# Attention scores from one product of 64 partitions per head, in two banks, in place of one product of two heads against keys in a block with zeros

## The chip, the cores and the metric

The kernel runs on one core of a Trainium2 chip. The metric is device time in microseconds (us) of one execution, and the figure of a kernel is the median of several runs. A second, profiled execution gives the trace: one record for each instruction of TensorE (PE for the products, PEld for its weight loads), VectorE (DVE), ScalarE (ACT), GpSimd (POOL) and for each transfer.

## The reference

Three stages follow each other: attention over keys and values that are averaged in groups of 8, a gated feed-forward block (moe) with a norm, and a second feed-forward block (moe2). Only the first is touched by the change.

```python
batch, n_heads, seq, head_dim = (4, 8, 576, 64)          # q, k, v
def _attn_ref(q, k, v):
    pool = 8; Sp = S // pool                              # 72 pooled positions
    scale = 1.0 / np.sqrt(D)
    k_p = k.reshape(B, H, Sp, pool, D).mean(axis=3)
    v_p = v.reshape(B, H, Sp, pool, D).mean(axis=3)
    scores = scale * np.matmul(q, k_p.transpose(0, 1, 3, 2))
    scores = scores - np.max(scores, axis=-1, keepdims=True)
    attn = np.exp(scores)
    attn = attn / (np.sum(attn, axis=-1, keepdims=True) + 1e-09)
    return np.matmul(attn, v_p)
# then moe on 2304 tokens x 512 (hidden 1536), then moe2 of the same sizes
```

## The kernel before

The 2304 tokens are cut into 18 sub-tiles of 128 tokens for the attention (`sub_steps(s)`). One batch has 576 tokens, so sub-tiles 4 and 13 hold the end of one batch in their first 64 rows and the beginning of the next in the other 64. The feed-forward block works on token tiles of 512, 256, 768 and 768, and its many products of 128 x 128 weights fill TensorE from about 36 us to the end. The attention of the later sub-tiles is strewn between them.

Pooled keys. For each batch `k_pool(p)` (L320) sums the keys of head pair p in groups of 8 into `kp` (DVE, 128 partitions: two heads of 64 dimensions each). `k_blocks(hh)` (L331) then copies the rows of one head of every pair, times 1/8, into `KB`, a tile of 128 x 4 x 144: rows 0 to 63 hold the first head of each pair in columns 0 to 71, rows 64 to 127 the second in columns 72 to 143, and the rest are zeros that GpSimd writes once at the start (L226). Two such tiles take turns over the batches.

Scores. `scores` (L407) makes one product for each head pair: the stationary operand is the queries of the pair (128 partitions x 128 tokens), the moving one the 144 columns of `KB`. So 4 products fill a sub-tile's 576 scores, pairs 0 and 1 in one PSUM bank, pairs 2 and 3 in the next. A straddling sub-tile makes 4 products for its first 64 tokens and 4 for the others. Each product in f32 shows in the trace as two instructions of weight load and product, so an ordinary sub-tile has 8 of each. Behind the scores DVE takes the maximum of each head (`top`, L434) and, from sub-tile 4 on, subtracts it (L436). In sub-tiles 0 to 3 TensorE subtracts it instead (`less`, L440). ACT takes the exponent (L452), and TensorE transposes the result (`turn`, L459).

Order. The order on the compute engines is written out by hand: `FIRST` and `SECOND` are lists of tokens, and each token issues one step. `S5.0` is the scores of sub-tile 5, `S5.1` the maximum, `S5.2` the exponent, `k0` to `k3` are `k_pool` of batch 0, `b0` and `b1` its `k_blocks`; `p`, `r` and `u` are the same steps of batches 1 to 3 (0 to 3 `k_pool`, 4 to 6 the values, 7 and 8 `k_blocks`, 9 the values' blocks). A `!` moves a step to another engine. Within one engine the instructions run in this order, whatever is ready. `laid_out` arranges the inputs on the host: it decides which two heads form a pair.

Of the kernel before, what the change touches and what calls it, by code (L numbers as in the profile page):

```python
# [45 lines left out]
Y10l! W11c M1.ca Fb00l W11l! S11.10 V11b O10a H11 M1.la! S11.11 S11.12 Y11c Y11l O10b Fd0 M0.la!
M0.e1! S12.2 S13.0 Ft1c M0.e2! O11a T1 S13.1 T0 Fd2 O11b T2 S13.2 M0.e3 T3 || S13.3 M0.1 M0.cs Ft1l
M1.1 M0.ls! M0.e4 M0.2 M1.e1 u9 S13.4 S12.3 M0.cr Fd1 Ft3c M0.p5 S12.4 M1.e2 M0.3 M0.lr! M1.3 M0.p1
Ft2c Fd3 Ft2l S13.5 M1.cs M0.cb M1.ls! M0.4 M1.2 Fb11c M1.p1 Ft3l Fb11l M2.ca M0.u2 M1.e4! M1.e3!
M2.la S13.6 M1.cr Ft4c M0.7 M0.d3 M0.d1 M1.4 M0.lb M1.lr! Ft4l M1.d1 S12.5 M2.e1! M1.u2 M0.5 M0.z1  # L50
M1.p5 S12.6 M2.3 M1.7 M2.e2! M1.6 M0.d2 M0.d5 M1.5 M2.cs M2.1 M2.e3 M1.cb M0.z2 M3.ca S14.0 M2.e4!
M2.ls! M0.d4 M3.e1! M1.lb! M2.2 M2.cr M1.z1 M1.d3 M2.p1 M2.6 M2.p5 M3.la! M3.e2! M3.cs M3.3 M2.4
M4.ca M1.d2 M1.d5 M2.d1 M2.lr M2.cb M3.1 M2.5 M2.u2 M2.lb M3.ls! M2.7 M3.e3 S14.1 M3.e4 M2.z1
M4.e1! M1.z2 M3.2 M4.e2! M4.la M2.d2 M3.cr M3.p1 M2.d3 M2.z2 M3.6 M3.d1 M3.z1 M1.d4 M4.cs S15.0
M2.d5 M4.3 M3.4 M3.lr! M4.1 M3.p5 M4.e4 M3.cb S15.1 M4.e3! S14.2 M4.cr M5.ca M3.u2 M4.ls! M3.lb
M2.d4 M5.e1 M4.lr! S14.3 M5.e2 M3.5 M4.2 M5.e3! S15.2 M4.p1 M3.d2 M3.7 M5.cs M3.d3 M4.d1 M5.e4
M4.p5 M3.z2 M5.ls M4.4 M6.ca M4.6 M5.la! M4.5 M3.d5 M5.3 M5.cr M6.la M5.2 M6.e1 M4.u2 S12.7 M6.e2!
# [96 lines left out]
def attention_moe_moe2(  # L154
# [1509 lines left out]
```

## Time and profile before

| | us |
|---|---|
| runs | 957.96, 960.32, 960.05 |
| median | 960.05 |
| the profiled execution | 960.59 |
| its span, first to last instruction | 958.9 |
| PE busy in the span | 933.3 |
| DVE busy | 631.6 |
| ACT busy | 485.6 |
| granted TensorE clock, mean | 0.994 of full |

The profiled execution took 960.59 us, of which 958.9 are the span and 1.7 lie around it. Engines overlap, so busy times don't add up to the span. A product's record reaches from its start to the modelled end of its way through the array; the next one may start long before that. The distance between two starts is therefore the better measure of what one product takes.

### The profile page before, as it was taken

To read this page: it belongs to the slowest core of one execution; us is meant where nothing else is said; L and a number is where in the kernel's file an instruction comes from. 1 tells how busy PE (TensorE), PEld (TensorE's weight loads), DVE (VectorE), ACT (ScalarE), POOL (GpSimd) and SP (SyncE) were. 2 spreads that over 40 slices of the span, in tenths; PEclk is the share of its full clock that TensorE was granted. 3 is DMA by queue.
4 is the path that set the end of the run, shared out by engine and by line. 5 is a ranking of instruction groups with operands and counts; after the bars stand their busy time and mean duration, and the time that the engine had idled before them with its cause. 6 is when DMAs were issued, how large, how long until landed. Compare 5 with 4: busy or idle time off the path is not lost. (4 is left out here: it accounts for less than half of the span.)

```text
span 958.9 us, 14761 instructions
## 1 busy us (share of the span) xinstructions
PE 933.3 (97%) x5242; PEld 854.0 (89%) x5242; DVE 631.6 (66%) x1119; ACT 485.6 (51%) x941; POOL 310.9 (32%) x291
## 2 busy tenths in 40 slices
PE   7899999999999999999989999999999999999998
PEld 6786676999999998999978899999999998888886
DVE  5889664778877867767856798766666675232221
ACT  3776643867675644666645565444434444322211
POOL 3312412653555322254322205443333433400000
PEclk9999999999999999999999999999999999999999
DMA  8577623543011163521474434344444336553431
GB/s 296 204 212 247 213 94 110 165 127 102 29 50 50 53 184 116 168 97 58 134 240 146 133 107 154 128 135 135 135 154 140 127 116 230 179 165 99 159 105 66
DMA packets 67945, 133.35 MB, mean 139 GB/s; under 512 B 7456, under 2 KB 31264, under 8 KB 67872
## 3 DMA queue, kind: packets, MB, share of 16 engines
q1 hardware_dynamic: 67728, 132.28, 42.4%
q8 instruction: 41, 0.67, 0.3%
q14 instruction: 32, 0.26, 0.1%
q10 hardware_dynamic: 144, 0.13, 0.0%
HBM read 93.06 MB, written 39.32 MB: 138 GB/s over the span
## 5 line engine op out<-in xcount | busy, mean ns | idle before, releaser
L1188 DVE TENSOR_TENSOR hl<-hf,hh 128x768 fp32r<-128x768 f32 x36 | 35.0, 976 | 91.7 <-ACT hh L1187 91.7
L1210 PE MATMUL o<-woh,hh 128*128 128x512 f32 x216 | 84.0, 389 | 0.0
L1210 PE MATMUL o<-wol,hh 128*128 128x512 f32 x216 | 84.0, 389 | 0.0
L1210 PE MATMUL o<-woh,hl 128*128 128x512 f32 x216 | 84.0, 389 | 0.0
L1187 ACT CAST hh<-hf 128x768 fp32r<-128x768 f32 x36 | 30.0, 839 | 85.3 <-PE o L1210 76.8
L1543 PE MATMUL o<-hh,wol 128*128 128x256 f32 (+1 forms) x192 | 66.0, 344 | 3.2 <-ACT hh L1527 1.9
L1543 PE MATMUL o<-hl,woh 128*128 128x256 f32 (+1 forms) x192 | 65.4, 340 | 1.1 <-DVE hl L1530 1.1
L1543 PE MATMUL o<-hh,woh 128*128 128x256 f32 (+1 forms) x192 | 65.4, 341 | 0.0
L647 POOL TENSOR_TENSOR w<-w,st 128x512 int32<-128x512 int32 x20 | 26.2, 1312 | 114.9 <-DVE w L640 68.7
L1115 ACT COPY p<-X 128x384 f32<-128x384 f32 x36 | 17.3, 481 | 88.1 <-PE X L1107 88.1
L679 POOL TENSOR_TENSOR wl<-wf,wh 128x512 fp32r<-128x512 f32 x26 | 34.7, 1340 | 56.6 <-ACT wh L675 55.5
L1210 PEld LDWEIGHTS o<-woh,hl 128*128 128x128 f32 x216 | 40.5, 188 | 8.5
L1210 PEld LDWEIGHTS o<-wol,hh 128*128 128x128 f32 x216 | 40.5, 188 | 8.4
L617 ACT ACTIVATE st<-st 128x512 int32<-128x512 uint32 x72 | 48.0, 667 | 0.0
L1210 PEld LDWEIGHTS o<-woh,hh 128*128 128x128 f32 x216 | 40.5, 188 | 8.3
L1543 PEld LDWEIGHTS o<-hh,wol 128*128 128x128 f32 x192 | 36.8, 192 | 8.0 <-ACT hh L1527 2.4
L697 PE MATMUL acc<-ht,wo 128*128 128x512 f32 (+1 forms) x112 | 43.5, 531 | 0.0
L647 POOL TENSOR_TENSOR wo<-wo,st 128x512 int32<-128x512 int32 x16 | 21.8, 1362 | 64.7 <-ACT p L1115 24.9
L1107 PE MATMUL X<-xh_t,rl 128*128 128x384 f32 x120 | 40.6, 338 | 1.6 <-ACT u L1115 1.6
L1543 PEld LDWEIGHTS o<-hl,woh 128*128 128x128 f32 x192 | 36.7, 191 | 5.8 <-DVE hl L1530 1.6
L1107 PE MATMUL X<-xh_t,sl 128*128 128x384 f32 x120 | 40.8, 340 | 0.5 <-ACT p L1115 0.5
L1143 DVE TENSOR_TENSOR u<-u,Y 128x384 f32<-128x384 f32 x36 | 19.8, 550 | 32.4 <-ACT u L1115 15.3
(255 smaller groups left out, 3160.8 us busy)
## 6 DMA issues: line engine op xcount, KB each, us to landing
hf<-h SPq DMA_DIRECT2D x36, 384.0 KB, 3.1
st<-in_moe_w_out_dram SPq DMA_DIRECT2D x24, 512.0 KB, 3.9
h<-p SPq DMA_DIRECT2D x60, 192.0 KB, 1.9
h<-u SPq DMA_DIRECT2D x60, 192.0 KB, 1.9
wo_again<-wd SPq DMA_DIRECT2D x36, 256.0 KB, 2.8
st<-in_moe_w_gate_dram SPq DMA_DIRECT2D x12, 512.0 KB, 4.0
st<-in_moe_w_val_dram SPq DMA_DIRECT2D x12, 512.0 KB, 4.3
wd<-wo SPq DMA_DIRECT2D x24, 256.0 KB, 2.1
```

The lines of the kernel that those rows point to most:

```text
L617: nc.scalar.activation(out=low, in_=low.bitcast(U32), func=AF.Copy, scale=2.0 ** -29)
L647: (nc.vector if boot["alt"] else nc.gpsimd).tensor_tensor(out=bits, in0=bits, in1=low, op=ALU.add)
L679: (nc.vector if boot["alt"] else nc.gpsimd).tensor_sub(wl, wf[ph, f, i], wh.bitcast(F32))
L697: nc.tensor.matmul(accs[c][:, cols], w[:, c, :], ht[:, :cols.stop - cols.start], start=(f == 0 and cols.start == 0), stop=(f == NF - 1),)
L1107: nc.tensor.matmul(dst[:, :HALF], w[:, c0 + c, :], x[:, c, :], start=(start and i == 0), stop=(stop and i == 5), skip_group_check=True,)
L1115: nc.scalar.copy(t, src[:, :HALF])
L1143: nc.vector.tensor_add(u2, u2, Y[:, :HALF])
L1187: nc.scalar.copy(hh, hf)
L1188: nc.vector.tensor_sub(hl, hf, hh.bitcast(F32))
L1210: nc.tensor.matmul(accs[i], x[:, sub], y, start=(f == 0 and j == 0), stop=(f == NF - 1 and j == 2),)
L1543: nc.tensor.matmul(dst, w[:, c, :], x, start=(f == 0 and j == 0 and at == 0), stop=(f == NF - 1 and j == 2), skip_group_check=True,)
```

## The change

Queries and pooled keys of one pair stay in one tile of 128 partitions, the first head of the pair in rows 0 to 63, the second in rows 64 to 127. For each pair and each of the two heads there is now a product of its own with 64 partitions: 128 tokens of stationary queries, 72 moving columns. The first head's scores go to bank 0, the second's to bank 1. A pair is now made of heads p and p + 4, not 2p and 2p + 1, which `laid_out` arranges, so that heads 0 to 3 are bank 0 as before. `KB` has no zeros any more and is half as large; `k_pool` writes it directly. `kp`, `k_blocks` (8 steps over the four batches) and the two clears on GpSimd are gone. The factor 1/8 moves into the scale of the exponent. A number that pads a pool of on-chip memory changes from 120 to 88 words.

```diff
-q0 K K K K K w0! k0 k1 k2 W q1 K k3 K q2 b1 b0 G S0.0@att S0.1 S1.0@acc0 S1.1 S0.8 l S1.8
+q0 K K K K K w0! k0 k1 k2 W q1 K k3 K q2 G S0.0@att S0.1 S1.0@acc0 S1.1 S0.8 l S1.8 S0.2a w1 t0!
...
-    QK_SCALE = 1.0 / float(D) ** 0.5
+    QK_SCALE = 1.0 / (POOL * float(D) ** 0.5)
...
     for i in range(2):
-        t = const.tile([P, NP, 2 * SP], F32, tag=f"KB{i}", name=f"KB{i}")
-        nc.gpsimd.memset(t, 0.0)
-        KB.append(t)
+        KB.append(const.tile([P, NP, SP], F32, tag=f"KB{i}", name=f"KB{i}"))
...
         def k_pool(p):
-            if p == 0:
-                box["kp"] = sm_p.tile([P, NP, SP], F32, tag="kp", name=f"kp_{b}")
             t, _ = queue.pop(p)
             v3 = t.rearrange("p (s r) -> p s r", r=POOL)
-            nc.vector.reduce_sum(out=box["kp"][:, p, :], in_=v3, axis=AX.X)
+            nc.vector.reduce_sum(out=KB[b % 2][:, p, :], in_=v3, axis=AX.X)
             load()
...
-        def k_blocks(hh):
-            rows = slice(hh * D, (hh + 1) * D)
-            dst = KB[b % 2][rows, :, hh * SP:(hh + 1) * SP]
-            if hh == 0 or b > 0:
-                nc.scalar.mul(dst, box["kp"][rows], 1.0 / POOL)
-            else:
-                nc.vector.tensor_scalar_mul(dst, box["kp"][rows], 1.0 / POOL)
...
                 for p in range(2 * b0, 2 * b1):
-                    c0 = (p % 2) * 2 * SP
-                    nc.tensor.matmul(
-                        box["sc"][off:off + cnt, p // 2, c0:c0 + 2 * SP],
-                        q_t[s][:, p, off:off + cnt], KB[b % 2][:, p, :],
-                        start=(s >= BOOT or p % 2 == 0), stop=(s >= BOOT),
-                        skip_group_check=True,
-                    )
+                    for i in range(2):
+                        rows = slice(i * D, (i + 1) * D)
+                        nc.tensor.matmul(
+                            box["sc"][off:off + cnt, i, p * SP:(p + 1) * SP],
+                            q_t[s][rows, p, off:off + cnt], KB[b % 2][rows, p, :],
+                            start=(s >= BOOT or p == 0), stop=(s >= BOOT),
+                            skip_group_check=True,
+                        )
...
-        shift(x_p, 120)
+        shift(x_p, 88)
```

From `FIRST` and `SECOND` only the tokens of `k_blocks` are taken out (`b0 b1`, `p7 p8`, `r7 r8`, `u7 u8`; what was 9 is now 7). No other token moves.

At the start, DVE before: the four sums of batch 0 (L329), one of the two block copies (L341; the other stands on ACT), then the negative identity and the first maximum.

```order
L329 TENSOR_REDUCE kp_140<-kv_6_127 128x72 [waits DMAHW1_49]
L329 TENSOR_REDUCE kp_140<-kv_5_129 128x72 [waits DMAHW2_49]
L329 TENSOR_REDUCE kp_140<-kv_xl 128x72 [waits DMAHW3_49]
L329 TENSOR_REDUCE kp_140<-kv_xl 128x72 [waits DMAHW4_49]
L341 TENSOR_SCALAR KB_105<-kp_140 64x4x72 [waits DVE_49,Pool_49]
L212 TENSOR_SCALAR nident<-ident 128x128 [waits Pool_49]
L434 TENSOR_REDUCE m_182<-sc_175 128x8 [waits PE_49]
```

And DVE after:

```order
L324 TENSOR_REDUCE KB_105<-kv_6_125 128x72 [waits DMAHW1_49]
L324 TENSOR_REDUCE KB_105<-kv_5_127 128x72 [waits DMAHW2_49]
L324 TENSOR_REDUCE KB_105<-kv_xl 128x72 [waits DMAHW3_49]
L324 TENSOR_REDUCE KB_105<-kv_xl 128x72 [waits DMAHW4_49]
L211 TENSOR_SCALAR nident<-ident 128x128 [waits Pool_49]
L421 TENSOR_REDUCE m_181<-sc_170 128x8 [waits PE_49]
```

The sums now write the keys' tile themselves, and the copy between is gone; what follows is the same.

TensorE at sub-tile 13, which straddles two batches, before: the end of one output product of the feed-forward block, the scores (64 tokens against the keys of one batch, 64 against the other's), and the next output product.

```order
L1361 MATMUL acc_1650<-hl_2434,woh_10_2398 128x256
L412 MATMUL sc_2495<-KB_105,q_1972 64x144 [waits DMAHW6_49,PE_49,Activation_49]
L412 MATMUL sc_2495<-KB_105,q_1972 64x144 x3
L412 MATMUL sc_2495<-KB_107,q_1972 64x144 x4
L1361 MATMUL acc_1560<-hh_2480,wol_11_2452 128x256 [waits Activation_49]
L1361 MATMUL acc_1560<-hh_2480,woh_11_2451 128x256
```

And TensorE after, at the same place:

```order
L1347 MATMUL acc_1675<-hl_2476,woh_10_2441 128x256
L399 MATMUL sc_2537<-KB_105,q_2008 64x72 [waits DMAHW6_49,PE_49,Activation_49]
L399 MATMUL sc_2537<-KB_105,q_2008 64x72 x7
L399 MATMUL sc_2537<-KB_106,q_2008 64x72 x8
L1347 MATMUL acc_1587<-hh_2522,wol_11_2494 128x256 [waits Activation_49]
L1347 MATMUL acc_1587<-hh_2522,woh_11_2493 128x256
```

Each product of 144 columns has become two of 72; its neighbours and its waits are the same. An ordinary sub-tile differs in the same way (4 rows of 128x144 become 8 of 128x72).

## Rows read from the trace of the kernel before

**Rows 1.** Page, parts 1 and 2: PE busy us, share, count; tenths in 40 slices.

```profile
PE 933.3 (97%) x5242; PEld 854.0 (89%) x5242; DVE 631.6 (66%) x1119; ACT 485.6 (51%) x941; POOL 310.9 (32%) x291
...
PE   7899999999999999999989999999999999999998
```

**Rows 2.** Stretches: length, busy us (count) by engine, granted clock, DMA share, GB/s.

```profile
12.00:36.00 24.00, 20.24 (x111) 17.42 (x112) 17.69 (x40) 15.39 (x36) 7.34 (x7) 0.86 0.66 234
36.00:100.00 64.00, 60.53 (x308) 47.65 (x307) 57.45 (x103) 46.02 (x79) 16.37 (x13) 1.00 0.74 236
...
170.00:250.00 80.00, 78.62 (x638) 77.38 (x638) 65.95 (x130) 59.51 (x118) 43.23 (x44) 1.00 0.38 114
250.00:350.00 100.00, 99.42 (x609) 98.28 (x608) 77.17 (x158) 62.67 (x129) 43.22 (x46) 1.00 0.20 66
```

**Rows 3.** Instructions of tile sc: count, ns min/median/max, first and last start, forms.

```profile
L412 PE MATMUL sc<-KB,q x160: 283/286/448, 8.8 to 323.7; 128*128 128x144 f32 x128, 128*64 128x144 f32 x32
```

**Rows 4.** PE timeline at sub-tile 12: start us, us, instruction, count.

```profile
225.89 0.28 PE L689 MATMUL v<-xl,wh 128*128 128x256 f32 x1
226.01 1.15 PE L412 MATMUL sc<-KB,q 128*128 128x144 f32 x8
226.90 0.38 PE L689 MATMUL g<-xh,wl 128*128 128x256 f32 x1
227.11 0.28 PE L689 MATMUL g<-xh,wh 128*128 128x256 f32 x1
```

**Rows 5.** PEld timeline, two weight loads of 128 columns before products of 65.

```profile
34.07 0.30 PEld L482 LDWEIGHTS av<-VB,eT 128*128 128x128 f32 x2 [0.59 <-ACT eT L464]
```

**Rows 6.** PE timeline at sub-tile 13, which straddles two batches.

```profile
233.31 0.28 PE L1361 MATMUL acc<-hh,woh 128*128 128x256 f32 x1
233.43 0.28 PE L1361 MATMUL acc<-hl,woh 128*128 128x256 f32 x1
233.63 1.74 PE L412 MATMUL sc<-KB,q 128*64 128x144 f32 x16
235.30 0.38 PE L1361 MATMUL acc<-hh,wol 128*128 128x256 f32 x1
235.53 0.28 PE L1361 MATMUL acc<-hh,woh 128*128 128x256 f32 x1
```

**Rows 7.** PEld timeline, sub-tile 4: the weight loads in flight at 41.67 to 41.70.

```profile
41.65 0.14 PEld L412 LDWEIGHTS sc<-KB,q 128*64 128x64 f32 x2
```

**Rows 8.** PE timeline, scores of sub-tiles 0 to 2 [idle before <- releaser].

```profile
8.79 1.25 PE L412 MATMUL sc<-KB,q 128*128 128x144 f32 x8 [0.32 <-ACT KB L339]
12.03 1.79 PE L412 MATMUL sc<-KB,q 128*128 128x144 f32 x8 [1.99 <-DMA q<-in_q_dram]
...
18.01 1.25 PE L412 MATMUL sc<-KB,q 128*128 128x144 f32 x8
```

**Rows 9.** PE timeline, places where PE waits behind scores.

```profile
43.72 0.52 PE L518 MATMUL xP<-ident,x 128*128 128x128 f32 x3 [0.87 <-DVE x L511]
...
74.29 0.50 PE L689 MATMUL g<-xh,wl 128*128 128x512 f32 x1 [1.31 <-ACT ht L788]
...
164.84 0.36 PE L689 MATMUL g<-xh,wl 128*128 128x256 f32 x1 [0.86 <-ACT ht L1321]
...
167.37 0.41 PE L459 MATMUL eP<-ident,E 128*128 128x128 f32 x2 [0.86 <-DVE E L436]
...
238.08 0.77 PE L459 MATMUL eP<-ident,E 128*128 128x128 f32 x5 [1.10 <-ACT E L452]
...
319.59 0.44 PE L1107 MATMUL X<-xh_t,bl 128*128 128x384 f32 x1 [0.58 <-DVE p L1413]
```

**Rows 10.** Line 339, the block copies on ACT: count, ns, first and last start.

```profile
L339 ACT ACTIVATE KB<-kp x7: 428/441/445, 8.3 to 226.1; 64x288 f32<-64x288 f32 x7
```

**Rows 11.** DVE and ACT timelines behind the scores of sub-tile 13.

```profile
235.41 0.76 DVE L434 TENSOR_REDUCE m<-sc 128x8 f32<-128x576 f32 x1 [0.17 <-PE sc L412]
...
236.31 1.13 ACT L254 COPY ev<-acc 128x256 f32<-128x256 f32 x3 [0.32 <-PE acc L1361]
```

More of the change, by code (lines that the diff above doesn't have):

```diff
@@ new lines @@
+Ft4c M0.7 M0.d3 M0.d1 M1.4 M0.lb M1.lr! Ft4l M1.d1 S12.5 M2.e1! M1.u2 M0.5 M0.z1 M1.p5 S12.6 M2.3
+M1.7 M2.e2! M1.6 M0.d2 M0.d5 M1.5 M2.cs M2.1 M2.e3 M1.cb M0.z2 M3.ca S14.0 M2.e4! M2.ls! M0.d4
+M3.e1! M1.lb! M2.2 M2.cr M1.z1 M1.d3 M2.p1 M2.6 M2.p5 M3.la! M3.e2! M3.cs M3.3 M2.4 M4.ca M1.d2
+M1.d5 M2.d1 M2.lr M2.cb M3.1 M2.5 M2.u2 M2.lb M3.ls! M2.7 M3.e3 S14.1 M3.e4 M2.z1 M4.e1! M1.z2 M3.2
+M4.e2! M4.la M2.d2 M3.cr M3.p1 M2.d3 M2.z2 M3.6 M3.d1 M3.z1 M1.d4 M4.cs S15.0 M2.d5 M4.3 M3.4
+M3.lr! M4.1 M3.p5 M4.e4 M3.cb S15.1 M4.e3! S14.2 M4.cr M5.ca M3.u2 M4.ls! M3.lb M2.d4 M5.e1 M4.lr!
@@ new lines @@
+N0.z1 N1.3 N1.cr Qe5 N0.d2 N0.d3 N1.lr! Jt4l N0.z2 N2.la! N1.1 N1.p5 N2.cs N1.p1 N1.5 N2.e4 N1.4
+N1.6 N2.ls! N2.e3 N1.cb N2.cr N0.d5 N2.2 N0.d4 N1.u2 N3.e1! N2.1 N1.7 N3.e2! N2.lr N3.e3! N1.d3
+N3.e4! N2.3 N2.p5 N3.cs N2.p1 N1.d2 N3.ca N2.d1 N1.lb N3.cr N2.4 N3.ls N2.5 N3.la! N2.u2 N1.d1
+N4.e1! N2.6 N1.z1 N3.3 N1.d5 N4.e2 N1.z2 N3.1 N4.ca N3.2 N2.cb N1.d4 N4.cs N3.lr! N2.lb! N2.7
+N4.ls! l N3.p1 N3.4 N2.d3 x0.0 N3.p5 N5.ca N2.d2 N3.d1 N4.e3! N5.la! N2.z1 N3.u2 N3.6 N4.la N3.cb
+N4.e4 N3.5 N4.2 N2.d5 N4.cr N2.z2 N4.1 N5.e1! N3.d2 N3.z2 N2.d4 N4.lr! N5.e2! N5.e4 N4.p1 N5.cs
@@ new lines @@
+x1.2 N9.d4 N10.d2 N9.d5 N10.3 N10.z2 N11.2 N10.cb N11.e4 N10.d3 N11.cr N10.lb N10.d1 N10.d4 N10.z1
+N11.lr! N11.1 N11.p5 N11.6 N11.p1 N11.4 N11.cb N11.u2 x0.3! x2.2 U0.f N11.5 N11.7 U0.w N10.d5
+N11.lb x1.3! U0.x N11.d2 U0.h1 N11.z2 N11.d3 N11.3 N11.d4 N12.6 U0.h0 U1.f U0.k0 U0.2 N11.d1 U0.3
+N11.z1 U1.w N11.d5 U1.h1 U1.x! U1.k1 U0.k1! U0.4 U0.0 x2.3 U1.h0 U0.5 U1.k0 U0.1 U2.f U2.h1 U1.5
+U2.w Zo U1.4 U2.k1! U2.x! U2.h0 x3.2 U3.f U1.1 Zb11c U1.3 Zb00c U2.k0 U1.2 U1.0 Z0.e1 U2.4 U2.0
+U2.5 U2.2 U3.w U3.h1 U3.h0 U4.f U2.3 Zb00l U3.x! U2.1 U3.k1 U4.w U3.4 U3.k0 U3.1 U3.3 U4.h1 U3.2
@@ L142 @@
+g12a S5.3@att g12b s10.1h c2 s12.0h l c0 o10 c0 s10.1l! c1 S5.4 h11 c3! v12a c1 c2 s11.0h a12
+S5.5@att c3! s12.0l! s11.0l v12b S4.7 g13a s12.1h S5.6 c2 o11 S5.7 h12 s11.1h c3! g13b a13 R4
+s11.1l! S4.9 S4.10@att v13a S4.11 v13b h13 s12.1l! S4.12 o12 S5.9 S5.10@att S5.11 S5.12 o13
 """.split()
@@ L352, in prep_steps @@
         steps += [lambda c=c: v_pool(c) for c in range(0, NV, 2)]
-        steps += [lambda h=h: k_blocks(h) for h in range(2)]
         if b == 0:
@@ L717, in attention_moe_moe2 @@
     name("w", prep[0][4:7])
[L718 to L719 removed]
+    name("t", prep[0][7:])
     name("p", prep[1])
```

194 lines of the change are left out of this document (85 added, 109 removed).

## Prediction

> **What bounds the kernel now.** I read the page first: TensorE is busy 933.3 of 958.9 us, and from the third of the 40 slices on its row shows nines with a few eights [rows 1]. By stretches it is busy 99.4 of 100 us from 250 to 350, 78.6 of 80 from 170 to 250, but 60.5 of 64 from 36 to 100 and 20.2 of 24 from 12 to 36 [rows 2]. So in the second half of the attention a change of TensorE's work moves the end one for one; before that there are waits of TensorE that can swallow a delay, and they have to be looked up one by one. The scores are 160 instructions between 8.8 and 323.7 us, 128 of full size and 32 in the two straddling sub-tiles [rows 3], that is 8 in each of 16 ordinary sub-tiles and 16 in each of two others.
>
> **What an ordinary sub-tile costs now.** At sub-tile 12 eight score instructions take 1.15 us, of which the last takes 0.286 [rows 3, 4]; so the seven distances are (1.15 - 0.286) / 7 = 0.123 us. The products ahead and behind join without a gap: from 226.01 to the second product behind, 227.11, it is 1.10 us, of which 0.12 is one step of those products [rows 4]. The scores thus occupy TensorE for 8 x 0.123 = 0.98 us.
>
> **What it will cost.** There will be 16 instructions with 72 columns and 64 partitions. No row shows a product of 64 partitions; the nearest rows are these.
> - The floor of one step. Where products have only 65 columns, two weight loads of 128 columns take 0.30 us together, of which one alone has 0.19: they start 0.11 us apart [rows 5]. A product of 72 columns streams in 72/144 of 0.12, or 0.06 us, so the weight load sets its step: 0.11, not 0.06.
> - Side by side or in turn. In the straddling sub-tiles the two halves use different 64 columns of the array, and 16 products take 1.74 us, that is (1.74 - 0.286) / 0.123 = 11.9 steps where 15 would be needed in turn [rows 3, 6]: the second half began beside the first when three of it were left. In the same overlap two weight loads together take 0.14 us [rows 7], so loads run side by side as well. I take that the two heads of a pair, in different rows of the array, do so too: 8 steps of 0.11.
> - The change of shape. Ahead of sub-tile 13 the last full product starts at 233.43 and streams as long as the steps of these products, 0.12 us (233.31 to 233.43), so until 233.55; the 128*64 products begin at 233.63, 0.08 to 0.09 later. Behind it the last score starts at 233.63 + 1.74 - 0.29 = 235.08 and streams 0.12, until 235.20; the next product begins at 235.30, 0.10 later, and its successor follows after 0.23 instead of 0.12 [rows 6]. So each change costs about 0.09 us of emptying and then one weight load that nothing hides, 0.11 for 128 columns.
>
> An ordinary sub-tile then takes 0.09 + 0.11 to get in, 7 x 0.11 + 0.06 for the products, 0.09 + 0.11 to get out: 1.23 us, 0.25 more than now. From below: without any cost of the change of shape it is 8 x 0.11 = 0.88, 0.10 less than now. From above: if all 16 follow each other, 15 x 0.11 + 0.06 + 0.40 = 2.11, 1.13 more. I take 0.25, since rows 6 and 7 stem from these very score products with one dimension of the array cut in half.
>
> [...]
>
> **Where the 0.25 counts.** Of the sixteen ordinary sub-tiles, 0 to 3 stand in the first 30 us. There TensorE comes from idle, so getting in is free and the first load is bare already (1.25 us where sub-tile 12 has 1.15) [rows 4, 8]; getting out makes 0.11 + 7 x 0.11 + 0.06 + 0.20 = 1.14 against 0.11 + 0.98 = 1.09. Sub-tile 0 is followed by 1.99 us of waiting for the queries of sub-tile 1 [rows 8], so it costs nothing. For 1 to 3, with a granted clock of 0.86 in this stretch [rows 2], I put +0.2 together, between 0 and 0.5. Sub-tile 5 is followed at 74.29 by a wait of 1.31 us for ACT, 6 and 7, which stand ahead of 164.84 and 167.37, by waits of 0.86 and 0.86, and 16 at 319.59 by one of 0.58 on a chain of DVE [rows 9]: these four are swallowed. Eight are left, 8 to 12, 14, 15 and 17: 8 x 0.25 = +2.0.
>
> **The straddling sub-tiles.** Sub-tile 13 changes shape already now: from the end of the stream before it (233.55) to the stream behind it (235.30 + 0.11) it is 1.86 us [rows 6]. With 64 partitions and 64 columns each product has a load of about 0.05 and a stream of 0.06, so 8 steps of 0.06 for each half; if the second half again begins when three are left, 7 steps later, it is 0.09 + 0.05 + 15 x 0.06 + 0.09 + 0.11 = 1.24: 0.62 less. Behind it TensorE waits 1.10 us for the exponent [rows 9], whose chain goes through the maximum on DVE (0.17 of waiting for these scores) and, on ACT, through three copies of output sums that wait for the products behind the scores [rows 11]. Those move up with TensorE, the maximum only by 0.17, so I count -0.5 (between -0.2 and -0.6). In sub-tile 4 the same gain ends in the 0.87 us for which TensorE waits for `x` at 43.72 [rows 9]: nothing.
>
> **The keys.** Seven block copies of 0.44 us on ACT go [rows 10], an eighth on DVE, and two clears on GpSimd. The first scores can start up to 0.5 us earlier (the copy released them at 8.79), but behind them stands the transfer of the queries [rows 8], whose place in SP's queue doesn't change: nothing. The pair of copies of batch 1 stands on ACT ahead of weight casts, not ahead of the `x` that TensorE waits for; the later ones run where TensorE has work. I take 0, at most -0.9 (two copies). The sums on DVE keep their size and places, and no new wait arises: the scores wait for DVE where they waited for ACT.
>
> **The sum** goes against the profiled execution: 960.59 + 2.0 - 0.5 + 0.2 = 962.3 us. That execution is 0.54 above the median, so the median should come to 961.8, +0.18%. The runs lie up to 2.4 us apart, so about 0.3% (2.9 us) is what a measurement here can tell from no change.
>
> **Rivals.**
> - *In turn* (slower). The heads of a pair don't run side by side, or their weight loads don't, so each step is 0.11 for one head. Then each ordinary sub-tile costs 1.13 more: 8 x 1.13 = 9.0; sub-tiles 6 and 7 keep 0.6 beyond their two waits, 16 keeps 0.55 beyond 0.58, 5 is still swallowed; 1 to 3 cost some 0.9 each, 2.7; sub-tile 13 has 0.14 + 31 x 0.06 + 0.06 + 0.20 = 2.26, 0.4 more. Sum +13.2, so 973.2. For it: no row has a product of 64 partitions. Against it: rows 6 and 7. It decides once a pair's step is over 0.13 us: (2.9 - 1.7) / (8 x 7) = 0.02 above 0.11.
> - *Partly side by side*. Steps of some 0.15 us, for instance because products of f32 come in twos for each head and the second head starts late. 0.28 more for each sub-tile: +2.2 on the eight and some more early, about 964.5.
> - *Cheap change of shape*. Cutting the rows empties nothing and hides the load: 8 x -0.10, sub-tile 13 -0.6, early -0.3, so -1.7 and 958.4. For it: only a cut of columns is shown to empty the array.
> - *Half the time*. If the step were set by the 72 columns, a sub-tile would take 0.49 + 0.40 = 0.89, 0.09 less: 8 x -0.09 - 0.5 - 0.2 = -1.4, 958.7. Against it stands row 5, where 65 columns still have steps of 0.11. [...]
> - That the change doesn't do what it says would be *in turn*: two products where there was one and nothing for it.
>
> **How the numbers follow.** Forecast 0.60, in turn 0.15, partly 0.08, cheap change 0.12, half 0.05. Predicted: 961.8. The range leaves out *in turn* and small ends of the rest: from 957.8 (958.4 and the lower bounds of keys) to 966.0 (*partly* with steps of up to 0.17). Slower by over 0.3%, above 962.9: in turn 0.15, partly 0.06, and 0.10 of the forecast's own 0.60, since 962.9 is only 1.1 away and the terms of the early sub-tiles and of the swallowed ones can add that: 0.31. Faster, below 957.2: 0.04 out of the two cheap cases. Within: 0.65.
>
> **What would show it.** In the trace after: 320 score instructions with 64 partitions; their starts in pairs a few ns apart with 0.11 us between pairs (forecast), or 0.11 between single ones (in turn), or 0.06 (half). Ahead of the first and behind the last 0.09 us of gap and then a step longer by 0.11, or none (cheap change). From the product ahead to the product behind 1.23 us for sub-tile 12, 1.24 for 13. The first scores earlier by 0.3 to 0.5 us with the second group still at 12.0; the waits at 74.3, 164.8, 167.4 and 319.6 shorter by about 0.25. The prediction is wrong if the row cut costs otherwise than the column cut, or if delays that I call swallowed come back on DVE or ACT.

## The result: 966.0 us, slower by 0.68%

| | before | after |
|---|---|---|
| median of the runs, us | 960.18 | 966.01 |
| runs, us | 957.96, 960.32, 960.05, 961.11 | 965.50, 966.13, 965.90, 967.91 |
| the profiled execution | 960.59 | 965.50 |
| its span | 958.9 | 963.7 |

The ratio is 1.0068, with a 95% interval of 1.0046 to 1.0090. The forecast was 961.8, with "within 0.3%" as the likeliest outcome. The late score products behave as forecast. Two other things come on top of them: where later tiles lie in on-chip memory (177 ns instead of 173 for each of 1008 later products), and TensorE's clock around sub-tile 4 (0.81 of full from 42 to 51 us, 1.00 before). Neither had a term in the sum.

Page of the kernel after, parts 1 and 2: busy us, share and count by engine, then TensorE's share in 40 slices.

```profile
PE 938.4 (97%) x5402; PEld 856.5 (89%) x5402; DVE 630.3 (65%) x1118; ACT 481.9 (50%) x934; POOL 309.3 (32%) x289
...
PE   7899999999999999999989999999999999999998
```

TensorE has 160 instructions more and is busy 5.1 us longer than in [rows 1]. ACT and DVE have given up their copies, but the row of nines hasn't changed.

The scores, by the tile `sc`: count, ns min/median/max, first and last start, forms.

```profile
L399 PE MATMUL sc<-KB,q x320: 222/272/327, 8.9 to 327.9; 64*128 64x72 f32 x128, 64*64 64x72 f32 x32
```

There are 320 of them with 64 partitions, as the change says; [rows 3] had 160 with 128.

TensorE at sub-tile 12 after: start us, us, instruction, count.

```profile
228.84 0.28 PE L676 MATMUL v<-xl,wh 128*128 128x256 f32 x1
229.05 1.11 PE L399 MATMUL sc<-KB,q 64*128 64x72 f32 x16
230.09 0.39 PE L676 MATMUL g<-xh,wl 128*128 128x256 f32 x1
230.31 0.28 PE L676 MATMUL g<-xh,wh 128*128 128x256 f32 x1
```

And its weight loads there.

```profile
229.05 0.97 PEld L399 LDWEIGHTS sc<-KB,q 64*128 64x128 f32 x16
230.09 0.19 PEld L676 LDWEIGHTS g<-xh,wl 128*128 128x128 f32 x1
230.20 0.19 PEld L676 LDWEIGHTS g<-xh,wh 128*128 128x128 f32 x1
```

And the loads of the scores there before.

```profile
225.90 1.04 PEld L412 LDWEIGHTS sc<-KB,q 128*128 128x128 f32 x8
```

From the product ahead to the second behind it is 1.47 us where [rows 4] has 1.22: +0.25. Sixteen loads take 0.97 us, of which one alone is 0.19, so seven steps make (0.97 - 0.19) / 7 = 0.11 us: the two heads of a pair run side by side, and the pairs follow each other in steps of 0.11, as the weight loads ahead of products of 65 columns do in [rows 5]. The change of shape shows at both ends. With the 0.12 of these products as its step, the product ahead would be followed at 228.84 + 0.12 = 228.96; the first score starts 0.09 later, and its load only with it, at 229.05, where the first load stands 0.11 ahead of its product before (225.90 and 226.01). The last pair starts at 229.05 + 1.11 - 0.27 = 229.89, and the second product behind it follows after 0.42, where it follows the last score after 227.11 - (226.01 + 1.15 - 0.29) = 0.24 in [rows 4]. So these scores with 64 rows have the 0.09 us at the way in that [rows 6] has for 64 columns (0.08 to 0.09). A pair takes 0.11 where one full product took 0.12, so the trace shows 1.1 times the speed.

Sub-tile 13 after, the same view.

```profile
236.64 0.28 PE L1347 MATMUL acc<-hl,woh 128*128 128x256 f32 x1
236.85 1.03 PE L399 MATMUL sc<-KB,q 64*64 64x72 f32 x32
237.81 0.38 PE L1347 MATMUL acc<-hh,wol 128*128 128x256 f32 x1
238.03 0.28 PE L1347 MATMUL acc<-hh,woh 128*128 128x256 f32 x1
```

Here it is 1.39 us from product ahead to second behind, where [rows 6] has 2.10: 0.71 less.

Where the time went is seen by following the same product in both traces: how much later does it start after than before, each by its own span? At 100 us 1.35 us, at 230 us 3.20, behind sub-tile 13 2.50, and then, with only four more score groups to come, 6.18 at 484 us. (At 494 us the kernel before has 3.4 us at half clock in its trace that the other lacks, so at the end only 5.05 are left; the runs, 5.8 apart, don't hang on this one stretch.) From 405 to 480 us TensorE makes nothing but products of 384 columns, on both sides. Stretch 405 to 480 us: length, busy us (count) by engine, granted clock, DMA share, GB/s; before:

```profile
405.00:480.00 75.00, 75.00 (x435) 74.96 (x434) 58.56 (x104) 46.86 (x100) 33.00 (x35) 1.00 0.32 102
```

and after:

```profile
405.00:480.00 75.00, 75.00 (x426) 75.00 (x425) 57.05 (x100) 47.15 (x100) 32.82 (x36) 1.00 0.32 106
```

Both are busy all the time at full clock, and nothing waits; yet 9 products fewer are made. Two of the count only reach in from the edges, so one step is 75 / 433 = 173 ns before and 75 / 424 = 177 ns after. There are 1008 such products (L1107 before, L1093 after) from 239 us to the end of this part at 485 us. What they compute, and with what, hasn't changed. In the same products of the second block (600 to 800 us) both kernels have 173.3 ns, by the starts in their traces.

### The profile page after: what moved, and what is told of

It reads as the page before. It is cut to its first block, busy times and chain, and to the rows that moved or that the text cites. A ratio compares the mean times of both kernels' runs of the same rounds, so it can differ in the third digit from the quotient of the medians.

```text
span 963.7 us, 15068 instructions
## 1 busy us (share of the span) xinstructions
PE 938.4 (97%) x5402; PEld 856.5 (89%) x5402; DVE 630.3 (65%) x1118; ACT 481.9 (50%) x934; POOL 309.3 (32%) x289
## 4 chain that ended last, share of the span: by engine, by line
PE 87%; DVE 4%; DMA 4%; ACT 3%; issue 1%; SPq 1%; POOL 0%; DVEq 0%; POOLq 0%; ACTq 0%
PE X L1093 24%; PE o L1196 15%; PE Y L1093 12%; PE o L1529 9%; PE Z L1093 6%; PE v L676 5%; PE g L676 4%; PE acc L684 4%; PE av L469 3%; PE acc L1347 1%; PE sc L399 1%; DMA hf<-h 1%; PE eP L446 1%; PE xP L505 1%; DMA q<-in_q_dram 1%
## 5 line engine op out<-in xcount | busy, mean ns | idle before, releaser
L1093 PE MATMUL X<-xh_t,rl 128*128 128x384 f32 x120 | 40.7, 339 | 1.1 <-ACT u L1101 1.1
L1093 PE MATMUL X<-xh_t,sl 128*128 128x384 f32 x120 | 40.9, 341 | 0.4 <-ACT p L1101 0.4
```

The source lines that it names most:

```text
L1093: nc.tensor.matmul(dst[:, :HALF], w[:, c0 + c, :], x[:, c, :], start=(start and i == 0), stop=(stop and i == 5), skip_group_check=True,)
```

## Experiment 1: is it where the tiles lie?

`KB` is half as large and `kp` is gone, so the tiles that are placed behind them on the same side of on-chip memory have moved. In the built programs the moving tiles of these products (`xh_...`, `xl_...`) lie 3456 bytes higher than before; the weights (`ah`, `al`, `sh`, ...) haven't moved. My theory was that the distance between the two makes the step. Four kernels part it from the scores.

All tiles back at their old places (but for ten small ones, `warm` and `ba`, which lie 1152 bytes higher), with the products per head:

```diff
-        KB.append(const.tile([P, NP, SP], F32, tag=f"KB{i}", name=f"KB{i}"))
+        kb = const.tile([P, NP, 2 * SP], F32, tag=f"KB{i}", name=f"KB{i}")
+        KB.append(kb[:, :, :SP])
...
+    sm_p.tile([P, NP, SP], F32, tag="kp", name="kp_pad")
...
-        shift(x_p, 88)
+        shift(x_p, 120)
```

> The changed kernel with every tile of on-chip memory back at the place that it has in the kernel before (the keys' tiles padded to their old size, an unused tile where kp stood, the pad at 120 words again). Theory of places: the 1008 products of 384 columns between 240 and 484 us are slower after the change (starts 176.7 ns apart instead of 173.6) only because their moving tiles have moved by 3456 bytes; so the step is 173.6 again and the time 966.0 - 1008 x 0.0031 = 962.9 us. Rival, the scores themselves or their instructions slow what follows: the step stays 176.7 and the time 966.0.

The moving tiles moved by a pad. With them go the weights `woh` and `wol` of the 144 output products of 256 columns (L1361 in the kernel before), and four early tiles by 512 bytes; the keys' tiles stay:

```diff
+    sm_p.tile([P, 96], F32, tag="spare", name="spare")
...
-        shift(x_p, 88)
+        shift(x_p, 120)
```

> The changed kernel with one unused tile of 96 words more, so that the moving tiles of the 384-column products have the remainder of the kernel before again when the address is divided by 512 bytes (96, where the changed kernel has 480), while the keys' tiles stay where the changed kernel has them. Theory of places, with the remainder as what counts: step 173.6 ns and 962.9 us. If the exact place counts and not its remainder, or if the scores are the cause: step 176.7 and 966.0.

The other way round, in the kernel before (the number of `shift(x_p, ...)` goes down by 32, so that all other tiles but `woh` and `wol` stay):

```diff
+    sm_p.tile([P, 32], F32, tag="spare", name="spare")
```

> The kernel before, with its old scores, and 32 unused words that move the moving tiles of the 384-column products down by 128 bytes, to the remainder of the changed kernel (480 of 512). Theory of places: the step goes from 173.6 to 176.7 ns and the time from 960.2 to 963.3 us with no change of the scores at all. Rival, the scores are the cause: 173.6 ns and 960.2.

And the products alone, with the block of zeros, the copies and all places as before (`laid_out` pairs the heads as after):

```diff
-                        q_t[s][:, p, off:off + cnt], KB[b % 2][:, p, :],
+                            box["sc"][off:off + cnt, i, p * SP:(p + 1) * SP],
+                            q_t[s][rows, p, off:off + cnt], KB[b % 2][rows, p, i * SP:(i + 1) * SP],
```

> The kernel before with the score products alone changed: one product of 64 partitions per head, in two banks, but keys still copied into the block with zeros, and all tiles at their old places. Theory: the scores alone cost 966.0 - 960.2 less the 3.1 us of places, so 962.9 us if the block copies are worth nothing, up to 963.5 if they are worth 0.6; the 384-column step stays at 173.6 ns, sub-tile 12 takes 1.47 us from product ahead to second product behind (1.22 before). Rival, the scores slow the later products: 966.0 and 176.7 ns.

| kernel | scores | moving tiles | median, us | ratio to before (960.62), 95% | products in 405 to 480 us |
|---|---|---|---|---|---|
| before | old | old | 960.62 | 1 | 435 |
| before, tiles moved | old | remainder as after | 964.05 | 1.0028 (1.0013 to 1.0043) | 427 |
| products alone | per head | old | 962.67 | 1.0023 (1.0008 to 1.0037) | 435 |
| after, all old places | per head | old | 963.42 | 1.0029 (1.0012 to 1.0047) | 435 |
| after, one pad | per head | old remainder | 963.92 | 1.0025 (1.0010 to 1.0039) | 434 |

The same stretch in the kernel before with its tiles moved:

```profile
405.00:480.00 75.00, 75.00 (x427) 75.00 (x426) 56.84 (x102) 46.66 (x99) 32.84 (x35) 1.00 0.32 105
```

and in the changed kernel with the pad:

```profile
405.00:480.00 75.00, 75.00 (x434) 74.97 (x433) 58.17 (x103) 47.93 (x101) 32.91 (x35) 1.00 0.33 109
```

The step goes with the place and not with the scores. A pad of 128 bytes makes the kernel before lose 0.28%, without a score touched. In its trace TensorE is 0.84 us later than in the kernel before at 240 us and 3.60 us at 484: 2.8 us. What is left for the scores and the keys is 0.23 to 0.29%, 2.2 to 2.8 us, with intervals from 0.08 to 0.47%, where the prediction had 1.7. The block copies are worth nothing that these runs can tell: without them (1.0025, 1.0029) it is no faster than with them (1.0023).

## Experiment 2: which distance is slow?

Four more pads in the kernel before (as above, with 64, 96, 16 and 48 words), and in the changed kernel the weights moved instead of the moving tiles (with them everything placed behind them on their side, 660 tiles in all):

```diff
+    cb_p.tile([P, 32], F32, tag="spare", name="spare", bufs=1)
```

> The kernel before with 64 unused words, so the moving tiles of the 384-column products lie 256 bytes lower (remainder 352 of 512, and 96 of 256 as in the kernel before). If the remainder by 256 bytes sets the step: 173.6 ns. If the remainder by 512 does: 176.7 ns or another value.

> The kernel before with 96 unused words, the moving tiles 384 bytes lower: remainder 224 of 512 and of 256, where 96 and 352 of 512 gave 173.6 ns and 480 gave 176.7. If the remainder by 256 counts, with the weights as they are: 176.7 ns. If 480 of 512 is special: 173.6.

> The changed kernel with 32 unused words ahead of the stationary tiles of these products, so that the weights lie 128 bytes higher (remainder 0 of 256 instead of 128) and the moving tiles stay at 480 of 512 (224 of 256). If the distance between weights and moving tile, by 256 bytes, sets the step: 173.6 ns, as the distance is again that of the kernel before (224). If the place of the moving tile alone does: 176.7 ns.

> The kernel before with 16 unused words: the moving tiles lie 64 bytes lower, 160 bytes of 256 above the weights, between the fast distances (224 and 0 of 256) and the slow one (96). If the slow distances begin at 128 or below: 173.6 ns for the 384-column step. If everything but 224 and 0 is slow: 176.7 ns.

> The kernel before with 48 unused words: moving tiles 192 bytes lower, 32 bytes of 256 above the weights. If the slow stretch of distances is around 96 alone: 173.6 ns. If distances from 0 up to 96 grow slow: between 173.6 and 176.7 ns or the latter.

Each was run once, which is enough for the step but not for the time. The stretch from 405 to 480 us; with 64 words:

```profile
405.00:480.00 75.00, 75.00 (x434) 74.98 (x434) 57.88 (x103) 46.95 (x100) 34.21 (x36) 1.00 0.32 107
```

with 96 words:

```profile
405.00:480.00 75.00, 75.00 (x426) 75.00 (x426) 57.26 (x102) 46.10 (x99) 32.89 (x35) 1.00 0.30 102
```

the changed kernel with the weights moved:

```profile
405.00:480.00 75.00, 75.00 (x434) 74.98 (x434) 57.98 (x103) 47.46 (x101) 32.90 (x35) 1.00 0.32 108
```

and the kernel before with 16 words, then with 48:

```profile
405.00:480.00 75.00, 75.00 (x434) 74.98 (x433) 58.39 (x105) 46.50 (x99) 33.07 (x36) 1.00 0.31 102
...
405.00:480.00 75.00, 75.00 (x428) 74.97 (x427) 57.27 (x103) 46.29 (x98) 33.01 (x36) 1.00 0.30 101
```

| kernel | moving tile, bytes mod 512 | weights | distance mod 256 | products |
|---|---|---|---|---|
| before | 96 | 128 | 224 | 435 |
| before, 64 words | 352 | 128 | 224 | 434 |
| after, weights moved | 480 | 256 | 224 | 434 |
| before, 16 words | 32 | 128 | 160 | 434 |
| before, 48 words | 416 | 128 | 32 | 428 |
| after | 480 | 128 | 96 | 426 |
| before, 32 words | 480 | 128 | 96 | 427 |
| before, 96 words | 224 | 128 | 96 | 426 |

The moving tile at 480 is slow with the weights at 128 and fast with them at 256, so its own place doesn't decide; the distance by 256 bytes orders all rows. 160 and 224 are fast (434 or 435 products) and 96 is slow (426 or 427). 32 wavers (428): by the starts, 173.9 ns from 240 to 280 us, 175.3 from 280 to 320 and 176.7 from 440 on. In the second block the weights lie at 480 and the moving tiles at 480 or 224, so the distance is 0, and it is fast there (173.3 ns). Why a distance is slow isn't shown. No distance but these was tried.

These rows alone can't tell the distance to the weights from the distance to anything else on the weights' side, since all of it moved together. The 144 output products of 256 columns can. There it is the weights (`woh`, `wol`) that the pads move, while the moving tiles stay. By the starts, their step is 116.9 to 117.2 ns at a distance of 32 (13 kernels), 117.5 at 160 (3), 118.3 at 224 (48 words) and 119.5 at 96 (16 words). So 96 is the slowest for them too, while 32, at which the products of 384 columns waver, is fast. And 96 is slow in the very kernel whose products of 384 columns, at 160, are fast: in these runs the step goes with the distance between a product's own two operands.

## Experiment 3: what of the scores' own loss is early, what late?

With the block of zeros kept, a sub-tile can have either kind of product; where an old one stands with the new pairing, heads 1 to 6 land in each other's places. All tiles lie as before. The condition is `s < 5`, `s >= 5`, `s == 4` or `s == 13`.

```diff
+                    if not (s < 5):
+                        c0 = (p % 2) * 2 * SP
+                        nc.tensor.matmul(
+                            box["sc"][off:off + cnt, p // 2, c0:c0 + 2 * SP],
+                            q_t[s][:, p, off:off + cnt], KB[b % 2][:, p, :],
...
+                        continue
                     for i in range(2):
```

> One product per head in two banks in sub-tiles 0 to 4 alone; sub-tiles 5 to 17 have the old product of 144 columns (with the new pairing of heads their scores of heads 1 to 6 stand in each other's places, so the output is not the reference's, but the work is that of the kernel before). All tiles at their old places. Theory: the part of the scores' cost that my sum missed is early. In the four traces with products per head the wait for x behind sub-tile 4 is 1.6 to 2.9 us instead of 0.87 to 1.12, and the granted clock stands at half for 3.4 us behind it, which no trace of the old scores shows there; so that half stretch appears again, the mean granted clock of the runs is about 0.993 to 0.994 (0.9967 in the kernel before), and the time is 960.6 + 1.0 = 961.6 us. By my prediction: +0.2, 960.8, and the clock as before.

> The counterpart: sub-tiles 0 to 4 with the old product (heads 1 to 6 in each other's places there, so the output is not the reference's), 5 to 17 with one product per head. Theory: no half stretch behind sub-tile 4, mean granted clock as before (0.996 to 0.997); sub-tile 12 takes 1.47 us instead of 1.22, sub-tile 13 1.39 instead of 2.10, and the time is 960.6 + 8 x 0.25 - 0.5 = 962.1 us, as the prediction counted this part. If the early part cost nothing: 963.2, the whole excess.

> Products per head in the straddling sub-tile 4 alone; in all others the old product (heads 1 to 6 in each other's places there, so the output is not the reference's). Theory: its scores take about 1.03 us of record instead of 1.74, TensorE then waits 0.7 us longer for x (1.6 instead of 0.9), and this longer wait is what lets the granted clock fall to half at 44 to 48 us: half stretch present, time 960.6 + 0 to 0.5, because a wait at 74 us swallows it. Rival: the early sub-tiles 0 to 3 bring x later; then no half stretch here.

> Products per head in the straddling sub-tile 13 alone (heads 1 to 6 in each other's places in all others, so the output is not the reference's). Theory and prediction: from the product ahead to the second one behind 1.39 us instead of 2.10, and TensorE 0.5 to 0.7 us earlier from 240 to 400 us than in the kernel before, by its start at 230. If the gain is lost again in the wait for the exponent behind: earlier by less than 0.2.

| products per head in | median, us | ratio to before (960.60), 95% | mean granted clock of the runs |
|---|---|---|---|
| sub-tiles 0 to 4 | 961.43 | 1.0012 (0.9996 to 1.0028) | 0.9941 |
| sub-tile 4 | 962.15 | 1.0011 (0.9995 to 1.0028) | 0.9942 |
| sub-tiles 5 to 17 | 961.39 | 1.0016 (1.0002 to 1.0029) | 0.9968 |
| none (before) | 960.60 | 1 | 0.9965 |

The late part costs 0.16%, 1.5 us, as forecast: 2.0 - 0.5; its interval is 0.2 to 2.8 us. Its trace, followed by the same product against the kernel before, has the steps one by one: each ordinary sub-tile +0.25 to +0.27, sub-tile 13 -0.71 with 0.10 given back behind it, and what 5, 6 and 7 together, and 16 add is taken back in the waits behind them (-0.46, -0.60, -0.27, the first two with something of their own; behind 7 another wait, at 171 us, then puts 0.62 on). Eight counted sub-tiles and sub-tile 13 make 8 x 0.26 - 0.61 = 1.5. With sub-tile 13 alone changed (one run), TensorE is 0.27 us ahead of the kernel before at 230 us and 0.86 ahead at 240: 0.59 kept.

The early part is not settled by its time, since both intervals reach below zero. Its clock says more: runs in which sub-tile 4 has products per head have 0.9941 and 0.9942, those without 0.9965 and 0.9968, each with a standard error of 0.0004 to 0.0006 (12 runs or more). Among the runs of one kernel a mean clock lower by 0.001 goes with about 0.5 us more (224 runs of ten kernels and the kernel before), so 0.0023 would be 1.2 us: an estimate, near the 1.1 to 1.2 measured. TensorE around sub-tile 4 in the kernel with sub-tile 4 alone:

```profile
39.67 0.72 PE L422 MATMUL sc<-KB,q 64*64 64x72 f32 x16
41.48 1.18 PE L422 MATMUL sc<-KB,q 64*64 64x72 f32 x16 [1.10 <-ACT KB L339]
44.24 1.94 PE L528 MATMUL xP<-ident,x 128*128 128x128 f32 x8 [1.58 <-DVE x L521]
```

and the stretch of 9 us there:

```profile
42.00:51.00 9.00, 7.42 (x47) 7.14 (x48) 6.91 (x18) 4.26 (x8) 0.00 (x0) 0.62 0.40 141
```

The same stretch with products per head in 5 to 17, so the old ones in sub-tile 4:

```profile
42.00:51.00 9.00, 8.76 (x61) 7.97 (x62) 8.56 (x15) 5.83 (x12) 1.18 (x1) 1.00 0.49 147
```

The scores of sub-tile 4 end sooner, `x` doesn't come sooner, and TensorE waits 1.58 us for it; in the kernel before it waits 0.87 [rows 9]. Behind the longer wait the granted clock is 0.62 on the mean of these 9 us (half clock for (1 - 0.62) x 9 / 0.5 = 6.8 of them), and eight small products of `xP` take 1.94 us instead of 1.29 (products per head in 5 to 17). In the 18 traces of this study the two go together without exception: behind a wait of 1.58 to 2.91 us (7 traces) the clock of this stretch is 0.62 to 0.81, behind none or one of up to 1.12 us (11 traces) it is 1.00. The half stretch begins 0.4 to 1.1 us behind the end of the wait in five of the seven, and at its beginning or in it in the two kernels of this experiment, where 1.1 us of waiting for `KB` stand ahead as well; so it is the idle time around sub-tile 4 and not this wait alone that it goes with. The traces by themselves don't show which comes first, since `x` also comes later in the seven (44.2 to 46.1 us) than in the others that wait for it (42.0 to 43.9). The clock of the runs with sub-tile 4 alone, in which nothing ahead of it differs from the kernel before, is the better evidence. The gain of sub-tile 4 isn't nothing, as I had it: it turns into a wait (1.58 us instead of 0.87), and with the wait comes a slower clock (0.62 instead of 1.00).

The changed kernel itself, the same place:

```profile
41.50 1.03 PE L399 MATMUL sc<-KB,q 64*64 64x72 f32 x32
...
44.30 1.75 PE L505 MATMUL xP<-ident,x 128*128 128x128 f32 x8 [1.76 <-DVE x L498]
```

## Experiment 4: filling the wait

If the idle time lets the clock fall, work in its place should keep it up. In the kernel with products per head in sub-tile 4 alone, the old four products of each half come first:

```diff
-                    if not (s == 4):
+                    if True:
...
-                        continue
+                for p in range(2 * b0, 2 * b1):
+                    if s != 4:
+                        continue
```

> In sub-tile 4 each half of the tokens gets the four old products first and then the eight products per head, which write over them; all other sub-tiles have the old product (heads 1 to 6 in each other's places there, so the output is not the reference's). So the short products are there, but TensorE works where it waited: about 2.8 us of scores instead of 1.0. Theory, that the longer wait for x behind the shortened scores lets the granted clock fall: the wait at 44 us shrinks below 0.5 us, no half stretch follows, the mean granted clock of the runs returns from 0.994 (products per head in sub-tile 4 alone) to 0.9965, and the time is 960.6 to 961.0 us. Rival, the products of 64 partitions themselves lower the clock: half stretch stays, 0.994, 962.

In the changed kernel with its pad of 96 words, the same with products of 144 columns that are written over:

```diff
+                for p in range(0, NP, 2) if s == 4 else ():
+                    for _ in range(2):
+                        nc.tensor.matmul(
+                            box["sc"][off:off + cnt, p // 2, 0:2 * SP],
+                            q_t[s][:, p, off:off + cnt], KB[b % 2][:, p:p + 2, :],
+                            start=True, stop=True, skip_group_check=True,
+                        )
```

> The changed kernel with 96 unused words (moving tiles of the 384-column products at the old remainder) and, in sub-tile 4, four more products of 144 columns ahead of the products per head of each half, which write over them; it keeps TensorE at work where it waited for x. Theory: of the three parts of the loss, the places (3.1 us) and the clock behind sub-tile 4 (about 1.3) are gone, and what is left is the products per head of the later sub-tiles: 960.8 + 1.3 = 962.1 us, mean granted clock about 0.9965, no half stretch at 43 to 50 us. Rival, the early part of the loss is not the clock: clock near 0.9965 but time still 963.4, as with the pad alone.

And as a control, the kernel before with its own products of sub-tile 4 made twice:

```diff
-                for p in range(2 * b0, 2 * b1):
+                for p in list(range(2 * b0, 2 * b1)) * (2 if s == 4 else 1):
```

> The kernel before with each score product of sub-tile 4 made twice, so that TensorE works where it waits for x at 43.7 us. Theory: there is no half stretch behind sub-tile 4 to be avoided in the kernel before, so nothing is gained: 960.8 us, within 0.5. If filling this wait by itself helps (the kernel that filled it with the products per head had 959.4): 959.5.

| kernel | wait for x, us | clock, 42 to 51 us | median, us | ratio to before, 95% | mean clock of the runs | of the kernel before beside them |
|---|---|---|---|---|---|---|
| sub-tile 4 per head | 1.58 | 0.62 | 962.15 | 1.0011 (0.9995 to 1.0028) | 0.9942 | 0.9965 |
| the same, filled | 0.47 | 1.00 | 959.43 | 0.9982 (0.9969 to 0.9996) | 0.9968 | 0.9957 |
| after, pad, filled | none | 1.00 | 963.25 | 1.0020 (1.0004 to 1.0036) | 0.9949 | 0.9957 |
| before, twice | none | 1.00 | 961.47 | 1.0000 (0.9987 to 1.0013) | 0.9969 | 0.9957 |

The filled kernel, TensorE and then the stretch:

```profile
41.52 0.72 PE L424 MATMUL sc<-KB,q 64*64 64x72 f32 x16
42.71 1.29 PE L530 MATMUL xP<-ident,x 128*128 128x128 f32 x8 [0.47 <-DVE x L523]
```

```profile
42.00:51.00 9.00, 8.30 (x65) 7.43 (x62) 8.59 (x15) 5.33 (x11) 0.49 (x1) 1.00 0.50 171
```

The short products are there and the clock is 1.00, so here it isn't they that lower it; with work in place of the wait it stays up. For the time the answer is nearly clear only in the first pair: 959.4 against 962.2, each with its own runs of the kernel before beside it; the intervals of the two ratios just touch. In the changed kernel the stretch behind sub-tile 4 is mended too, but the time, +0.20% with 0.04 to 0.36, holds both the 0.14% of the theory and the 0.25% of the rival, and the mean clock comes back most of the way, from 0.0033 below the kernel before (0.9934 against 0.9967, pad alone) to 0.0008 (0.9949 against 0.9957). Its trace has half-speed stretches elsewhere in the first 36 us (11.7 to 18.6 and 32.2 to 35.6). Such stretches also stand there in kernels with the old scores, in some traces and not in others. But all seven traces with products per head in sub-tiles 0 to 3 have one between 11 and 20 us, four of them of 6.8 us; of the other eleven five have one, of 3.4 us. On the mean of 0 to 20 us the granted clock is 0.83 in `after_places`, `after_pad96` and `products_alone`, and 0.91 in the changed kernel as in the kernel before and in `before_pad32`. Whether the early sub-tiles lower the clock there too wasn't tested. So how much of the early loss of the changed kernel is the clock behind sub-tile 4 stays open. That the first filled kernel is faster than before wasn't repeated by the control, which does the same for the old scores and gains nothing. No version with the reference's output beat the kernel before.

Both heads of a pair in one bank wasn't tried.

## Why the prediction was wrong, and where it was right

- *The ordinary sub-tile*, +0.25: measured +0.25 to +0.27, with each of its parts (pairs side by side, a step of 0.11, a gap of 0.09 ahead, a first load that starts with its product). Right, and so *in turn* and *half the time* fall by the step, *cheap change of shape* by the 0.09. That a cut of rows costs the 0.09 of a cut of columns was an estimate from [rows 6], and the trace after bears it out. (The 11.9 steps that it read out of the old overlap are 11.8; nothing hangs on that.)
- *Where it counts*: right for the late ones and for 5 and 16, which waits swallow. For sub-tiles 6 and 7 no single trace decides. In the changed kernel they add 0.51 us, and the waits of 0.86 and 0.86 [rows 9] are 1.07 and 0.76 behind them; by 171 us, one wait later, 0.14 of it is left (+1.57 ahead of them, +1.71 then). With products per head from 5 on it is 0.53. But over the same stretch traces with the old scores in 6 and 7 differ from the kernel before by -0.20 to +0.83, 0.27 on the mean of the eleven (that kernel's 0 among them), and the seven with products per head there by 0.32 on the mean, so the delay is swallowed as far as these traces can tell. Of 1 to 3, put at +0.2, sub-tiles 2 and 3 add 0.08 and 0.04 and lose it again; what 1 adds can't be parted from its wait.
- *Sub-tile 13*: -0.71 instead of -0.62, and -0.6 kept instead of -0.5. The load of about 0.05 us in its sum was an estimate for which no row stands; in the trace after, the 32 loads there take 0.88 us and start in steps of 0.05 to 0.06 from pair to pair within each half. The wait behind it for the exponent grew only from 1.10 [rows 9] to 1.19 us.

The waits of TensorE in the changed kernel that answer to those of [rows 9], behind sub-tiles 6 and 7, 13 and 16:

```profile
167.13 0.36 PE L676 MATMUL g<-xh,wl 128*128 128x256 f32 x1 [1.07 <-ACT ht L1307]
...
169.56 0.74 PE L446 MATMUL eP<-ident,E 128*128 128x128 f32 x5 [0.76 <-DVE E L423]
...
240.67 0.77 PE L446 MATMUL eP<-ident,E 128*128 128x128 f32 x5 [1.19 <-ACT E L439]
...
323.70 0.44 PE L1093 MATMUL X<-xh_t,bl 128*128 128x384 f32 x1 [0.27 <-DVE p L1399]
```

The one behind sub-tile 5, 1.31 us before, is gone, and the last has shrunk by the 0.3 that sub-tile 16 added.

- *Sub-tile 4*, put at nothing: this step failed. The gain does end in the wait for `x`, but the wait grew from 0.87 to 1.76 us and the clock behind it fell (0.81 instead of 1.00 from 42 to 51 us); the sum had no term for the clock. Its price is 1.1 us by the runs, with an interval from -0.5 to 2.7, so it is shown by the clock of the runs and not by their time.
- *The keys*, put at nothing, at most -0.9: the copies are indeed worth nothing. But this step failed in what it didn't list, and it is the larger error: it costed the instructions that go with `k_blocks` and `kp`, not the memory that they free. That moved the moving tiles of 1008 later products, which I had in the diff as a number that pads a pool. 2.8 us, of which the sum had none.
- *The first scores*, forecast 0.3 to 0.5 us earlier: they start at 8.90 where [rows 8] has 8.79, and the second group at 12.77, not 12.03. Both hang on transfers: the copy is gone, but in this trace keys of the first batch came to DVE's sums 0.68 us later than in the kernel before, whose line is the first here, and the sums end at 8.88:

```profile
5.99 0.75 DVE L329 TENSOR_REDUCE kp<-kv 128x72 f32<-128x576 f32 x1 [1.01 <-DMA kv<-in_k_dram]
...
6.67 0.75 DVE L324 TENSOR_REDUCE KB<-kv 128x72 f32<-128x576 f32 x1 [1.61 <-DMA kv<-in_k_dram]
7.41 1.47 DVE L324 TENSOR_REDUCE KB<-kv_xl 128x72 f32<-128x576 f32 x2
...
8.90 1.11 PE L399 MATMUL sc<-KB,q 64*128 64x72 f32 x16
12.77 1.11 PE L399 MATMUL sc<-KB,q 64*128 64x72 f32 x16 [2.75 <-DMA q<-in_q_dram]
```

- *The sum*: 1.7 us forecast. The runs give 1.5 for the late scores (ratio 1.0016), 1.2 for the early ones (1.0012) and 2.7 for the places (1.0028), together 5.4; the change itself measured 5.8 by the medians (1.0046 to 1.0090 by the ratio). The three add up within their intervals. The rival *partly side by side*, which lay nearest in time, had the wrong mechanism. That its 964.5 is nearer than the forecast's 961.8 is luck.

## What to carry to other kernels

Here a tile that became smaller moved the tiles placed behind it, and the moved tiles cost this kernel 2.7 us, as much as the scores themselves (1.5 + 1.2): compare the step of the same products far away from the edit, and put the places back with a pad before judging it. Time saved right ahead of a wait can go into the wait: at sub-tile 4 alone the wait for `x` grew from 0.87 to 1.58 us and TensorE's clock from 42 to 51 us was 0.62 instead of 1.00, while at sub-tile 13 0.6 of the 0.71 us were kept. In this kernel products of half the partitions gained where TensorE already changed shape (sub-tile 13, -0.71 us), and lost where each group had to pay for it (+0.25 in an ordinary sub-tile).

## What the hardware showed that I had not expected

- In these traces products of 384 columns start in steps of about 173.4 ns (the kernel before, 405 to 480 us) or 176.7 ns (the kernel after), by the distance between the place of the moving tile and that of the weights modulo 256 bytes: 0, 160 and 224 fast, 96 slow, 32 now one and now the other (the table of Experiment 2; 0 in the second block). The slow step isn't even: in the changed kernel the steps run 180, 175, 177 and 175 ns in turn, in a period of four products that takes no notice of which tiles they read. The output products of 256 columns also have their slowest step at 96, 119.5 ns against 117.0 at 32. Products of 512 columns lie at a distance of 0 in the kernels before and after, so the two traces show no other step of theirs.
- In the 7 traces in which TensorE waits 1.58 to 2.91 us at about 44 us, 3.4 or 6.8 us at half clock lie around that wait; in the 11 in which it waits up to 1.12 us or not at all there is no such stretch (granted clock from 42 to 51 us: 0.62 to 0.81 against 1.00). In five of these it waits twice, 0.96 to 1.21 us for `KB` and 1.11 or 1.12 us for `x` shortly behind, and keeps its clock.
- At sub-tile 12 of the changed kernel the two products of a pair, in different rows of the array, start 6 to 7 ns apart, and their weight loads run side by side: 16 loads in 0.97 us, of which one alone takes 0.19.
